# Windowed attention and ReGLU feed-forward: first q and k loads divided between two queues by partition half, tile 1 in two halves, wider weight pieces, and work reordered around the first output

## The chip, the cores and the metric

The kernel runs on one core of a Trainium2 chip. The time is device microseconds of one execution; a figure with three runs is their median. TensorE (PE) multiplies, VectorE (DVE) and ScalarE (ACT) work on the results, GpSimd (POOL) converts inputs to 16 bits, and SyncE (SP) and ACT each have a queue that issues transfers between the chip's memory (HBM) and the core's buffer (SBUF, 128 partitions).

## The reference

Attention in a causal window of 64 positions over q, k, v of 8 batches, 8 heads, 576 positions and 64 values, then a feed-forward layer on the 4608 tokens of width 512:

```python
scores = scale * np.matmul(q, k.transpose(0, 1, 3, 2))
mask = (rel >= 0) & (rel < window)            # window = 64
attn = softmax(np.where(mask, scores, -1e9))
x = np.matmul(attn, v)                        # heads side by side: (4608, 512)
gate = np.maximum(x @ w_gate, 0.0)            # w_gate, w_val: (512, 1536)
val = x @ w_val
return (gate * val @ w_out)                   # w_out: (1536, 512)
```

All inputs and the output are float32; the matmuls take 16-bit operands.

## The kernel before

**Attention units.** The 4608 tokens are cut into 24 units of 192 (three to a batch); u0 is the first. A unit's k, q and v are converted (`u_cast`, mostly on POOL), k and q transposed on DVE (`u_trans`, 4 instructions), and multiplied to scores (`u_st`, 32 matmuls into four PSUM tiles). ACT takes the exponential (`u_exp`, 4), DVE multiplies with the band mask (`u_mask`, 4), and PE forms sums and outputs (`u_pv`, 32 matmuls, each on half of the array's columns). ACT copies them out (`u_copy`, 4), and DVE makes the reciprocal and the normalised rows `xt` (`u_sum`, `u_back`, `u_norm`).

**Feed-forward tiles.** Before, tiles 0 and 1 hold 512 and 256 tokens and ten more hold 384 (`sizes`, line 66). For each of 12 blocks f of the hidden width and each of `wg` and `wv`, four matmuls make a PSUM tile `h` (line 323); ACT applies the relu (L314), DVE multiplies the two (`g_sb`, L317). Then, for each 128 tokens, 12 matmuls make `op` (L366), which ACT copies out. The four PSUM tiles of `f_ps` are shared by `h`, `op` and u1's scores.

**Loads.** `qk_load(b)` issues a batch's k and q as eight transfers: for each of them four groups g, a group filling 32 partitions (0 to 31, 32 to 63, 64 to 95, 96 to 127) with pieces of 512 bytes. For batch 0, even g go to SP's queue and odd g to ACT's (line 150). Then come v0 to v2, twelve chunks of `wg` and `wv` (512 KB each, pieces of 1 KB, lines 130 to 132), six of `wo` (pieces of 2 KB), batch 1's q and k, and v3 to v5, all on SP's queue. Six staging tiles `stg` take the weights; POOL converts each chunk.

**Order.** `Weaver` is a heap of planned times: program order on each engine is the order in which closures are popped, and `plan_unit` gives each step of a unit a planned time. Engines run their own instructions in that order and wait for data. Before, `ffn(0)` first makes f = 0 and 1 for the 384 tokens of u0 and u1 (`early`), then waits for u2, which fills the tile's last 128 tokens; `ready` stands ahead of each tile's other matmuls.

Of the kernel before, what the change touches and what calls it, by code (L numbers as in the profile page):

```python
# [9 lines left out]
FP32 = mybir.dt.float32  # L10
FP16 = mybir.dt.float16
# [31 lines left out]
def kernel(  # L43
# [79 lines left out]
    def w_load(wt, src, j, at):  # L123
        sr = src.rearrange("(c p) n -> p c n", p=128)
        if wt is wo:
            stg = stage.tile([128, 2, 512], FP32, name="stg", tag="stg")
            nc.sync.dma_start(stg, sr[:, 2 * j:2 * j + 2])
            dst = wo[:, 2 * j:2 * j + 2]
        else:
            stg = stage.tile([128, 4, 256], FP32, name="stg", tag="stg")  # L130
            nc.sync.dma_start(stg, sr[:, :, 256 * j:256 * j + 256])
            dst = wt[:, :, 256 * j:256 * j + 256]
# [13 lines left out]
    def qk_load(b):  # L146
        for name, src in (("k", k), ("q", q)):
            nat = a_in.tile([128, 2, UB, 3, 128], FP32, name=name + "n", bufs=2)
            for g in range(G):
                eng = nc.scalar if b == 0 and g % 2 else nc.sync  # L150
                eng.dma_start(  # L151
                    nat[32 * g:32 * g + 32].rearrange("p h u m e -> p (h u m) e"),
                    src[b, 2 * g:2 * g + 2].rearrange("h (m i j) d -> i (h m) (j d)", i=32, j=2))
            for i in range(UB):
                units.setdefault(UB * b + i, {})[name] = nat[:, :, i]

# [143 lines left out]
    def span(t):  # L300
        return sizes[t] * 23.4 / 384 + (1.8 if t == 0 else 3.6)

    def ready(t):
        while normed[0] * U < starts[t] + sizes[t]:
            W.pop()

    def ffn(t):
        n = sizes[t]
        xt = xt_tile(t)
        g_sb = g_sb_p.tile([128, NF, 512], FP16, name="g_sb")  # L310
        done = set()
# [4 lines left out]
        def gate(f, r_sb, h2):  # L316
            nc.vector.tensor_tensor(g_sb[:, f, 0:n], r_sb[:, 0:n], h2[:, 0:n], MUL)  # L317
            done.add(f)

        def hidden(h, wt, f, c0, c1):  # L320
            w_need(wt, f // 2)
            for c in range(NC):
                nc.tensor.matmul(h[:, c0:c1], wt[:, c, f * 128:f * 128 + 128], xt[:, c, c0:c1],  # L323
                                 start=(c == 0), stop=(c == NC - 1))
            W.clock += 4 * (c1 - c0) / 2400.0

        early = {}
        if t == 0:
            while normed[0] < 2:
                W.pop()  # L330
            for f in range(2):
                for i, wt in enumerate((wg, wv)):
                    early[f, i] = f_ps.tile([128, 512], FP32, name=f"h{i}", tag="h")
                    hidden(early[f, i], wt, f, 0, 2 * U)
        ready(t)

        for f in range(NF):
            for i, wt in enumerate((wg, wv)):
                W.advance(W.clock)
                if (f, i) in early:  # L340
                    h = early[f, i]
                    hidden(h, wt, f, 2 * U, n)
                else:
                    h = f_ps.tile([128, 512], FP32, name=f"h{i}", tag="h")
                    hidden(h, wt, f, 0, n)
                if i == 0:
                    r_sb = f_sb.tile([128, 512], FP32, name="r_sb")
# [4 lines left out]
        def evac(sub, op):  # L352
            o_sb = f_sb.tile([128, DM], FP32, name="o_sb")
            nc.scalar.copy(o_sb, op)  # L354
            nc.sync.dma_start(out[bass.ds(starts[t] + sub * 128, 128)], o_sb)

        for sub in range(n // 128):
            op = f_ps.tile([128, DM], FP32, name="op", tag="h")
            ss = bass.ds(sub * 128, 128)
            for f0 in range(0, NF, 4):  # L360
                W.advance(W.clock)
                for f in range(f0, f0 + 4):
                    while f not in done:
                        W.pop()
                    w_need(wo, f // 2)
                    nc.tensor.matmul(op, g_sb[:, f, ss], wo[:, f],  # L366
                                     start=(f == 0), stop=(f == NF - 1))
                W.clock += 4 * 512 / 2400.0
            W.at(W.clock, lambda sub=sub, op=op: evac(sub, op))

    with tc.manual_schedule():
        qk_load(0)
# [12 lines left out]
        for c in wo_chunks:
            W.at(t_load, lambda c=c, at=t_land: w_load(*c, at))
            t_load, t_land = t_load + 1.45, t_land + 1.45
        W.at(t_load, lambda: qk_load(1))
        for u in range(3, 6):
            W.at(t_load, lambda u=u: v_load(u))  # L390
# [44 lines left out]
```

## Time and profile before

| | us |
|---|---|
| median of 3 runs (lowest, highest) | 370.93 (369.5, 372.52) |
| the profiled execution, its own time | 371.01 |
| its span, first to last instruction | 369.2 |
| PE busy in the span | 333.5 (90%) |
| DVE, ACT, POOL busy | 239.5, 178.5, 94.3 |

Between the span and the execution's own time lie 1.8 us. The page cuts the span into 40 slices of 9.2 us; a digit is a busy share in tenths. A wait is idle time of an engine ahead of an instruction, put down to what released it. The chain of waits follows the work that ended last backwards, from each step to what it waited for. Matmuls overlap, so the distance between their starts is their cost, and the duration shown of one is longer.

### The profile page before, as it was taken

The numbers are of one execution on the slowest core, as the hardware profiler recorded it, in microseconds if no ns is written. First come the engines' busy times: TensorE is split into PE (matmuls) and PEld (weight loads), VectorE is DVE, ScalarE is ACT, GpSimd is POOL, SyncE is SP. The second block draws the span as 40 slices with busy tenths as digits, with TensorE's granted clock in tenths as the row PEclk, the third lists the DMA queues.
The fourth block names the chain that finished last, engine by engine and source line by source line (L and its number), as shares of the span: only waits on it lengthen the run. The fifth ranks groups of instructions, "written<-read, shape, count | busy, mean of one in ns | idle before, by whom it ended". The sixth has DMA issues, their size and how long they took to land.

```text
span 369.2 us, 7893 instructions
## 1 busy us (share of the span) xinstructions
PE 333.5 (90%) x3136; PEld 190.4 (52%) x3136; DVE 239.5 (65%) x439; ACT 178.5 (48%) x375; POOL 94.3 (26%) x114
## 2 busy tenths in 40 slices
PE   0154999698999999999999999999999999999996
PEld 0152544376465555565565555555555555555552
DVE  0598643968787578487587587588587487494330
ACT  1092332546556446545555555555554654653331
POOL 1486733604313222005213221006124121000000
PEclk9995999989999999999999999999999999999999
DMA  9999999995498520696696510694795600101102
GB/s 158 210 315 348 379 204 180 237 183 114 116 187 113 151 51 3 160 181 119 156 185 113 145 30 28 161 183 100 167 186 93 173 3 28 59 2 45 42 1 85
DMA packets 96901, 49.79 MB, mean 135 GB/s; under 512 B 47712, under 2 KB 90720, under 8 KB 96864
## 3 DMA queue, kind: packets, MB, share of 16 engines
q1 hardware_dynamic: 94496, 48.11, 63.2%
q10 hardware_dynamic: 2368, 1.18, 2.0%
q8 instruction: 24, 0.39, 0.5%
q14 instruction: 13, 0.11, 0.1%
HBM read 39.85 MB, written 9.44 MB: 134 GB/s over the span
## 4 chain that ended last, share of the span: by engine, by line
PE 84%; DVE 9%; DMA 4%; ACT 1%; issue 1%; ACTq 0%; DVEq 0%
PE h L323 51%; PE op L366 23%; PE pv L235 6%; DMA qn<-in_q_dram 4%; PE st L208 3%; DVE p L224 3%; DVE xt L270 2%; DVE sT L253 2%; DVE rs L261 1%; DVE qT L194 1%; ACT xs L248 1%; DVE rT L255 1%; DVE kT L194 0%; ACTq L151 0%; DVE g_sb L317 0%
## 5 line engine op out<-in xcount | busy, mean ns | idle before, releaser
L317 DVE TENSOR_TENSOR g_sb<-r_sb,h 128x384 f16<-128x384 f32 (+2 forms) x144 | 77.8, 546 | 74.8 <-PE h L323 73.5
L323 PE MATMUL h<-xt,wg 128*128 128x384 f16 (+3 forms) x584 | 119.2, 327 | 3.1 <-DVE xt L270 3.0
L323 PE MATMUL h<-xt,wv 128*128 128x384 f16 (+3 forms) x584 | 119.0, 327 | 0.3 <-DVE g_sb L317 0.3
L314 ACT ACTIVATE r_sb<-h 128x384 f32<-128x384 f32 (+2 forms) x144 | 71.6, 498 | 76.7 <-PE h L323 66.8
L366 PE MATMUL op<-wo,g_sb 128*128 128x512 f16 x432 | 97.0, 379 | 1.1 <-DVE g_sb L317 1.1
L323 PEld LDWEIGHTS <-wg 128*128 128x128 f16 x584 | 55.9, 99 | 43.3 <-issue 6.8
L323 PEld LDWEIGHTS <-wv 128*128 128x128 f16 x584 | 56.5, 99 | 38.0 <-issue 1.1
L366 PEld LDWEIGHTS <-g_sb 128*128 128x128 f16 x432 | 41.3, 98 | 49.4 <-issue 1.3
L220 ACT ACTIVATE p<-st 128x512 f16<-128x512 f32 x96 | 52.2, 607 | 11.3 <-PE st L208 11.1
L248 ACT COPY xs<-pv 128x384 f32<-128x384 f32 x96 | 39.5, 501 | 25.0 <-PE pv L235 25.0
L224 DVE TENSOR_TENSOR p<-p,mask 128x512 f16<-128x512 f16 x96 | 45.4, 492 | 9.0 <-ACT p L220 7.9
L354 ACT COPY o_sb<-op 128x512 f32<-128x512 f32 x36 | 21.1, 587 | 60.7 <-PE op L366 60.7
L182 POOL CAST k<-kn 128x768 f16<-128x768 f32 x24 | 23.1, 964 | 81.0 <-DMA kn<-in_k_dram 65.3
L235 PE MATMUL pv<-p,v 128*64 128x128 f16 x384 | 25.8, 232 | 10.3 <-DVE p L224 10.1
L182 POOL CAST q<-qn 128x768 f16<-128x768 f32 x23 | 20.2, 878 | 57.8 <-DMA qn<-in_q_dram 30.7
L175 POOL CAST v<-vn 128x1024 f16<-128x1024 f32 x16 | 17.2, 1076 | 66.6 <-PE pv L235 48.4
L194 DVE STREAM_TRANSPOSE kT<-k 128x384 f16<-128x384 f16 x48 | 27.7, 590 | 9.7 <-POOL k L182 8.7
L253 DVE STREAM_TRANSPOSE sT<-xs 128x768 f32<-128x768 f32 x24 | 23.1, 961 | 15.8 <-ACT xs L248 15.8
L208 PE MATMUL st<-qT,kT 32*128 32x128 f16 x768 | 16.8, 223 | 17.3 <-DVE qT L194 17.3
L194 DVE STREAM_TRANSPOSE qT<-q 128x384 f16<-128x384 f16 x48 | 26.6, 582 | 7.0 <-POOL q L182 3.8
L235 PEld LDWEIGHTS <-v 128*64 128x64 f16 x384 | 17.7, 115 | 19.1 <-issue 16.9
L235 PE MATMUL pv<-p,ones 128*64 128x128 f16 x384 | 25.1, 229 | 0.0
(26 smaller groups left out, 123.6 us busy)
## 6 DMA issues: line engine op xcount, KB each, us to landing
vn<-in_v_dram SPq DMA_DIRECT2D x40, 256.0 KB, 5.3
out_dram<-o_sb SPq DMA_DIRECT2D x36, 256.0 KB, 2.0
kn<-in_k_dram SPq DMA_DIRECT2D x30, 288.0 KB, 7.9
qn<-in_q_dram SPq DMA_DIRECT2D x30, 288.0 KB, 9.2
stg<-in_moe_w_gate_dram SPq DMA_DIRECT2D x6, 512.0 KB, 7.8
stg<-in_moe_w_val_dram SPq DMA_DIRECT2D x6, 512.0 KB, 8.1
stg<-in_moe_w_out_dram SPq DMA_DIRECT2D x6, 512.0 KB, 7.5
vn<-in_v_dram SPq DMA_DIRECT2D x8, 128.0 KB, 8.2
```

The lines of the kernel that those rows point to most:

```text
L182: nc.gpsimd.tensor_copy(c16, src)
L194: nc.vector.transpose(dst.rearrange("p h (m i j) -> p h m j i", i=32, j=2), src)
L208: nc.tensor.matmul(d["st"][g][:, (2 * hh + w) * 128:(2 * hh + w + 1) * 128], kT[rows, dh, hh, ks + 128 * w:ks + 128 * w + 128], d["qT"][ro ...
L220: nc.scalar.activation(d["p"][g].rearrange("p h c -> p (h c)"), d["st"][g], ACT.Exp, scale=scale)
L224: nc.vector.tensor_tensor(p, p, mask.rearrange("p w c -> p (w c)")[:, None, :].to_broadcast([128, 2, 256]), MUL)
L235: nc.tensor.matmul(pv[64 * e:64 * e + 64, s, 64 * w:64 * w + 128], d["v16"][:, w, 2 * g + e] if s == 0 else (ones0 if u % UB == 0 and w == ...
L248: nc.scalar.copy(d["xs"][:, g], d["pv"][g])
L253: nc.vector.transpose(sT.rearrange("p g b c -> p g (b c)"), d["xs"][:, :, 1])
L314: nc.scalar.activation(r_sb[:, 0:n], h1[:, 0:n], ACT.Relu)
L317: nc.vector.tensor_tensor(g_sb[:, f, 0:n], r_sb[:, 0:n], h2[:, 0:n], MUL)
L323: nc.tensor.matmul(h[:, c0:c1], wt[:, c, f * 128:f * 128 + 128], xt[:, c, c0:c1], start=(c == 0), stop=(c == NC - 1))
L366: nc.tensor.matmul(op, g_sb[:, f, ss], wo[:, f], start=(f == 0), stop=(f == NF - 1))
```

## The change

Names of units, tiles and blocks are as above.

- **First loads.** Batch 0's k and q: groups 0 and 1 (partitions 0 to 63) go to SP's queue, groups 2 and 3 (64 to 127) to ACT's. All batches issue g in the order 0, 2, 1, 3.
- **Weights.** A chunk of `wg` or `wv` is now 256 rows by 512 columns, in pieces of 2 KB, where it was 512 rows by 256 columns. Its size and the number of chunks stay. Four chunks serve f = 0 to 3, where two served f = 0 and 1.
- **Later loads.** v2 stands behind the first four weight chunks. Batch 1's q and k come in two goes: the first third (what u3 needs) in 16 small transfers, then v3, then the rest in 16, then v4 and v5.
- **Tiles.** All twelve have 384 tokens, two units each. Tile 1's hidden part is done in two halves of 192 (u2, then u3). Between them stands tile 0's output, now f by f over three `op` tiles at once (`output_by_rows`), where it was one `op` after another.
- **u2** has later planned times: its masks stand behind the normalisation of u1, its `pv` behind f = 0 and 1 of tile 0.
- **`heat`:** 14 matmuls of 256 columns on the mask, whose result is not read, behind u2's scores and ahead of tile 0.

```diff
-    sizes = [512, 256] + [384] * 10
+    TT = 2 * U
...
-            stg = stage.tile([128, 4, 256], FP32, name="stg", tag="stg")
-            nc.sync.dma_start(stg, sr[:, :, 256 * j:256 * j + 256])
+            cs, ns = slice(2 * (j % 2), 2 * (j % 2) + 2), slice(512 * (j // 2), 512 * (j // 2) + 512)
+            dst, part = wt[:, cs, ns], sr[:, cs, ns]
+        stg = stage.tile([128, 2, 512], FP32, name="stg")
+        nc.sync.dma_start(stg, part)
...
+    def queue(b, g):
+        return nc.scalar if b == 0 and g >= G // 2 else nc.sync
...
-                eng = nc.scalar if b == 0 and g % 2 else nc.sync
...
+            for i in range(G):
+                g = i // 2 + 2 * (i % 2)
+                rows = slice(32 * g, 32 * g + 32)
+                if blocks is None:
+                    queue(b, g).dma_start(
...
+                else:
+                    m0, m1 = blocks
+                    for h in range(2):
+                        queue(b, g).dma_start(
+                            nat[rows, h, m0:m1],
...
+    def output_by_rows(t):
+        ops = [op_tile() for _ in range(TT // 128)]
+        for f in range(NF):
+            W.advance(W.clock)
+            for sub, op in enumerate(ops):
+                out_mm(t, op, sub, f)
...
-        plan_unit(2, 18.3, (7.6, 10.9, 13.7), (9.0, 12.8), 1.6, 3.8, 5.3, 6.2, 7.7, 0.4)
-        plan_unit(3, 51.0, (44.5, 47.5, 48.5), (46.5, 49.0), 0.8, 1.5, 3.4, 4.5, 6.4, 0.5)
...
+        plan_unit(2, 18.3, (7.6, 10.9, 24.5), (9.0, 12.8), 1.6, 5.5, 8.0, 9.0, 10.4, 0.4)
+        plan_unit(3, 50.0, (44.0, 46.5, 47.5), (45.5, 48.2), 0.8, 1.5, 3.4, 4.5, 6.4, 0.5)
...
+        heat = f_ps.tile([128, 512], FP32, name="heat", tag="h")
+        for _ in range(14):
+            nc.tensor.matmul(heat[:, 0:256], mask[:, 0], mask.rearrange("p w c -> p (w c)"),
+                             start=True, stop=True)
...
+        ready(2)
+        hidden(0, 0, TT)
+        ready(3)
+        hidden(1, 0, U)
+        output_by_rows(0)
+        ready(4)
+        hidden(1, U, TT)
+        output(1)
```

On DVE, from u1's normalisation (`sT`, `rT`, `rs`, `xt`; u0's stands ahead of it, behind the eight masks of u0 and u1) to what follows, before:

```order
L253 STREAM_TRANSPOSE sT<-xs 128x768
L255 RECIPROCAL rT<-sT 128x24
L224 TENSOR_TENSOR p<-p,mask 128x512
L261 STREAM_TRANSPOSE rs<-rT 128x768
L224 TENSOR_TENSOR p<-p,mask 128x512 x2
L270 TENSOR_TENSOR xt<-xs,rs 128x4x192
L224 TENSOR_TENSOR p<-p,mask 128x512
L253 STREAM_TRANSPOSE sT<-xs 128x768
```

and now:

```order
L271 STREAM_TRANSPOSE sT<-xs 128x768
L273 RECIPROCAL rT<-sT 128x24
L279 STREAM_TRANSPOSE rs<-rT 128x768
L285 TENSOR_TENSOR xt<-xs,rs 128x4x192
L242 TENSOR_TENSOR p<-p,mask 128x512 x4
L331 TENSOR_TENSOR g_sb<-r_sb,h_459 128x384
```

Three masks of u2 stood inside u1's normalisation and the fourth behind it; all four now stand behind it, and the first gate comes ahead of u2's normalisation.

On SP's queue, from the `wo` chunks to the next batch's loads, before:

```order
L127 DMA stg<-in_moe_w_out_dram 128x2x512 x6
L151 DMA kn<-in_k_dram 32x18x128 x4
L151 DMA qn<-in_q_dram 32x18x128 x4
L164 DMA vn<-in_v_dram 64x8x64
L164 DMA vn<-in_v_dram 128x8x64 x5
L355 DMA out_dram<-o_sb 128x512 x3
```

and now:

```order
L131 DMA stg<-in_moe_w_out_dram 128x2x512 x6
L170 DMA kn<-in_k_dram 32x3x128 x8
L170 DMA qn<-in_q_dram 32x3x128 x8
L182 DMA vn<-in_v_dram 64x8x64
L182 DMA vn<-in_v_dram 128x8x64
L170 DMA kn<-in_k_dram 32x6x128 x8
L170 DMA qn<-in_q_dram 32x6x128 x8
L182 DMA vn<-in_v_dram 128x8x64 x4
```

The same bytes are moved in 32 transfers where eight did it, u3's part first, v3 between the two goes.

On DVE, around u3, before (k_725 and q_742 are u4's, k_867 is u5's; the twelve gates of tile 0 and u3's own transposes stand ahead):

```order
L194 STREAM_TRANSPOSE kT_95<-k_725 128x2x3x2x32
L224 TENSOR_TENSOR p<-p,mask 128x512 x2
L194 STREAM_TRANSPOSE kT_95<-k_725 128x2x3x2x32
L224 TENSOR_TENSOR p<-p,mask 128x512 x2
L194 STREAM_TRANSPOSE qT<-q_742 128x6x2x32 x2
L253 STREAM_TRANSPOSE sT<-xs 128x768
L255 RECIPROCAL rT<-sT 128x24
L261 STREAM_TRANSPOSE rs<-rT 128x768
L194 STREAM_TRANSPOSE kT_95<-k_867 128x2x3x2x32
L270 TENSOR_TENSOR xt<-xs,rs 128x4x192
L317 TENSOR_TENSOR g_sb<-r_sb,h_955 128x256
```

and now (k_857 and q_882 are u4's, k_1028 is u5's; the gates ahead are those of tile 1's first half):

```order
L331 TENSOR_TENSOR g_sb<-r_sb,h_894 128x192
L212 STREAM_TRANSPOSE kT_95<-k_857 128x2x3x2x32
L242 TENSOR_TENSOR p<-p,mask 128x512 x3
L212 STREAM_TRANSPOSE kT_95<-k_857 128x2x3x2x32
L242 TENSOR_TENSOR p<-p,mask 128x512
L212 STREAM_TRANSPOSE qT<-q_882 128x6x2x32 x2
L271 STREAM_TRANSPOSE sT<-xs 128x768
L273 RECIPROCAL rT<-sT 128x24
L279 STREAM_TRANSPOSE rs<-rT 128x768
L285 TENSOR_TENSOR xt<-xs,rs 128x4x192
L212 STREAM_TRANSPOSE kT_95<-k_1028 128x2x3x2x32
```

The order around u3 stays nearly the same; what moved is what stands ahead of it, the gates of a 384-token tile 0 and of half a tile 1 in place of those of a 512-token tile 0.

## Rows read from the trace of the kernel before

**Rows 1.** The page: span, PE's busy tenths and its granted clock in 40 slices.

```profile
span 369.2 us, 7893 instructions
PE   0154999698999999999999999999999999999996
PEclk9995999989999999999999999999999999999999
```

**Rows 2.** The chain of waits, first 90 us: start, length, what.

```profile
2.41 13.02 DMA qn<-in_q_dram
...
29.39 0.60 DVE p L224
...
30.88 0.95 DVE p L224 x2
31.83 1.71 DVE xt L270
...
38.32 0.98 DVE xt L270
...
82.25 1.01 PE pv L235 x32
```

**Rows 3.** DMA issues by line: queue, count, KB of one, median us to landing.

```profile
kn<-in_k_dram ACTq DMA_DIRECT2D x2, 288.0 KB, 6.6
```

**Rows 4.** Stretches: bounds, length, busy PE, PEld, DVE, ACT, POOL; clock, DMA share, GB/s.

```profile
7.00:8.00 1.00, 0.00 (x0) 0.00 (x0) 0.00 (x0) 0.00 (x0) 0.00 (x0) 1.00 1.25 174
...
11.00:12.00 1.00, 0.00 (x0) 0.04 (x1) 1.00 (x3) 0.00 (x0) 0.54 (x2) 1.00 1.23 286
...
24.00:34.00 10.00, 2.91 (x71) 2.22 (x68) 9.86 (x13) 4.98 (x12) 7.29 (x8) 0.67 1.10 348
41.00:45.00 4.00, 4.00 (x21) 1.82 (x19) 2.06 (x4) 1.27 (x3) 3.09 (x4) 1.00 1.05 386
48.00:57.00 9.00, 9.00 (x43) 4.05 (x42) 3.71 (x6) 2.98 (x5) 2.38 (x3) 1.00 1.24 187
```

**Rows 5.** PE in order of time: start, us from first start to last end, what.

```profile
35.34 1.46 PE L323 MATMUL h<-xt,wg 128*128 128x384 f16 x4
...
64.68 0.63 PE L208 MATMUL st<-qT,kT 32*128 32x128 f16 x32
65.23 2.76 PE L366 MATMUL op<-wo,g_sb 128*128 128x512 f16 x12
...
74.75 0.64 PE L323 MATMUL h<-xt,wg 128*128 128x256 f16 x4 [2.70 <-DVE xt L270]
75.18 1.06 PE L323 MATMUL h<-xt,wv 128*128 128x256 f16 x4
...
78.59 0.60 PE L323 MATMUL h<-xt,wv 128*128 128x256 f16 x4
79.03 0.60 PE L323 MATMUL h<-xt,wg 128*128 128x256 f16 x4
...
97.11 0.81 PE L323 MATMUL h<-xt,wg 128*128 128x384 f16 x4 [0.29 <-DVE xt L270]
...
98.41 0.82 PE L323 MATMUL h<-xt,wv 128*128 128x384 f16 x4
99.07 0.81 PE L323 MATMUL h<-xt,wg 128*128 128x384 f16 x4
...
357.61 7.93 PE L366 MATMUL op<-wo,g_sb 128*128 128x512 f16 x36
```

**Rows 6.** SP's queue in order of time: start, length of the issues, what.

```profile
0.81 0.93 SPq L151 DMA_DIRECT2D kn<-in_k_dram  x2
...
42.20 5.80 SPq L151 DMA_DIRECT2D kn<-in_k_dram  x4
```

**Rows 7.** DVE's gates by form: line, operation, shape, count; busy us, mean ns, idle before.

```profile
L317 DVE TENSOR_TENSOR g_sb<-r_sb,h 128x384 f16<-128x384 f32 x120 | 64.7, 545 | 59.9 <-PE h L323 59.2 <-ACT r_sb L314 0.4
...
L317 DVE TENSOR_TENSOR g_sb<-r_sb,h 128x256 f16<-128x256 f32 x12 | 4.9, 406 | 4.1 <-PE h L323 3.4 <-ACT xs L248 0.7
```

More of the change, by code (lines that the diff above doesn't have):

```diff
@@ L65 @@
     scale = 1.0 / float(D) ** 0.5
-    sizes = [512, 256] + [384] * 10
-    starts = [sum(sizes[:i]) for i in range(len(sizes))]
-    assert sum(sizes) == NT
+    TT = 2 * U
+    assert NT % TT == 0 and TT % 128 == 0
     consts = ctx.enter_context(tc.tile_pool(name="consts", bufs=1))
@@ L297, in plan_unit, with ready, hidden @@
         W.at(T + norm + 2.0, lambda: u_norm(u))
[L300 to L304, printed above, removed]
+    gs = {}
+    def ready(n):
+        while normed[0] < n:
             W.pop()
-    def ffn(t):
-        n = sizes[t]
+    def hidden(t, c0, c1):
+        if t not in gs:
+            gs[t] = g_sb_p.tile([128, NF, TT], FP16, name="g_sb"), set()
+        g_sb, done = gs[t]
         xt = xt_tile(t)
-        g_sb = g_sb_p.tile([128, NF, 512], FP16, name="g_sb")
-        done = set()
+        n = c1 - c0
         def relu(r_sb, h1):
@@ L316, in gate @@
         def gate(f, r_sb, h2):
[L317 to L335, printed above, removed]
+            nc.vector.tensor_tensor(g_sb[:, f, c0:c1], r_sb[:, 0:n], h2[:, 0:n], MUL)
+            if c1 == TT:
+                done.add(f)
         for f in range(NF):
@@ L339, in ffn @@
                 W.advance(W.clock)
[L340 to L345, printed above, removed]
+                w_need(wt, f)
+                h = f_ps.tile([128, 512], FP32, name=f"h{i}", tag="h")
+                for c in range(NC):
+                    nc.tensor.matmul(h[:, 0:n], wt[:, c, f * 128:f * 128 + 128], xt[:, c, c0:c1],
+                                     start=(c == 0), stop=(c == NC - 1))
+                W.clock += 4 * (n + 7) / 2400.0
                 if i == 0:
-                    r_sb = f_sb.tile([128, 512], FP32, name="r_sb")
+                    r_sb = f_sb.tile([128, TT], FP32, name="r_sb")
                     W.at(W.clock, lambda r_sb=r_sb, h=h: relu(r_sb, h))
@@ L350, in ffn, with out_mm, out_evac, evac @@
                     W.at(W.clock, lambda f=f, r_sb=r_sb, h=h: gate(f, r_sb, h))
-        def evac(sub, op):
+    def out_mm(t, op, sub, f):
+        g_sb, done = gs[t]
+        while f not in done:
+            W.pop()
+        w_need(wo, f)
+        nc.tensor.matmul(op, g_sb[:, f, bass.ds(sub * 128, 128)], wo[:, f],
+                         start=(f == 0), stop=(f == NF - 1))
+        W.clock += 519 / 2400.0
+    def out_evac(t, op, sub):
+        def evac():
             o_sb = f_sb.tile([128, DM], FP32, name="o_sb")
             nc.scalar.copy(o_sb, op)
[L355 to L369, printed above, removed]
+            nc.sync.dma_start(out[bass.ds(t * TT + sub * 128, 128)], o_sb)
+        W.at(W.clock, evac)
+    def op_tile():
+        return f_ps.tile([128, DM], FP32, name="op", tag="h")
+    def output(t):
+        for sub in range(TT // 128):
+            op = op_tile()
+            for f in range(NF):
+                if f % 4 == 0:
+                    W.advance(W.clock)
+                out_mm(t, op, sub, f)
+            out_evac(t, op, sub)
+    def output_by_rows(t):
+        ops = [op_tile() for _ in range(TT // 128)]
+        for f in range(NF):
+            W.advance(W.clock)
+            for sub, op in enumerate(ops):
+                out_mm(t, op, sub, f)
+        for sub, op in enumerate(ops):
+            out_evac(t, op, sub)
     with tc.manual_schedule():
+        qk_tiles(0)
         qk_load(0)
@@ L385 @@
[L385 to L390, printed above, removed]
+        chunks = [(wt, src, 2 * j + i) for j in range(3)
+                  for wt, src in ((wg, moe_w_gate), (wv, moe_w_val)) for i in range(2)]
+        chunks += [(wo, moe_w_out, j) for j in range(6)]
+        t_load, t_land = 6.0, 17.5
@@ L404 @@
+        ready(2)
[6 more added lines that the diff above has]
+        output(1)
+        for t in range(2, NU // 2):
+            ready(2 * t + 2)
+            hidden(t, 0, TT)
+            output(t)
         W.drain()
```

76 lines of the change are left out of this document (40 added, 36 removed).

## The prediction

> **What bounds the kernel now.** I read the page first. The span is 369.2 us; PE is near nine tenths busy in every slice from the fifth on, but for slices 8 and 10 [rows 1]. PE therefore sets the time, and a change can gain only ahead of its dense stretch and in the holes up to about 100 us. The granted clock says where PE, though busy, ran slowly: slice 4 stands at half, slice 9 below full [rows 1].
>
> The chain of waits says what is late at the start: for 13.02 us it is the first q, until 15.43; then DVE, whose normalisation of u1 ends at 31.83 + 1.71 = 33.5 with u2's masks inside it; then u2, whose last rows `xt` end at 39.30 [rows 2]. PE in order of time gives the marks that I count between. Tile 0 starts at 35.34, its first four matmuls taking 1.46 (half clock, since 0.81 is the usual), and tile 2 starts at 97.11 [rows 5]. From tile 2 on both kernels have the same tiles, units and order of work, so I forecast when tile 2 starts.
>
> In the kernel before, what PE does between the marks costs, by the distance between starts: four matmuls of 384 columns 0.66 (98.41 to 99.07), of 256 0.44 (78.59 to 79.03), so 0.22 for each 128; a unit's scores 0.55 (64.68 to 65.23); 36 output matmuls 7.93 [rows 5]; a unit's `pv` 1.01 [rows 2]. Tile 0 of 512 (24 x 0.88 = 21.1), tile 1 of 256 (24 x 0.44 = 10.6), 72 output matmuls (15.9), three scores and three `pv` (4.7) make 52.3, of 97.11 - 35.34 = 61.8. So 9.5 us are lost there: some 2 in tile 0's cold start and its wait for u2, 2.7 waiting for u3 at 74.75 [rows 5], 1.7 in the half clock right behind it (four groups from 75.18 to 78.59 take 3.41 and not 1.75) [rows 5], and some 3 in smaller waits on DVE.
>
> **The change part by part.**
>
> *First loads.* Eight transfers of 288 KB [rows 3] are 2.36 MB; in 13.02 us [rows 2] that is 181 GB/s. Both queues begin in partitions 0 to 63 and then both go to 64 to 127. The rate is 174 GB/s in the stretch from 7 to 8 and 286 from 11 to 12 [rows 4]. I read the second as a moment at which the queues, a transfer apart, wrote to different halves; no row says so. If halves are the limit, the new split holds the better rate throughout. Bounds: 181 (no gain) and 286 (8.3 us). I take 250, two thirds of the way, since short drops at the ends of transfers should remain: 9.4 us, a gain of **3.6** (0 to 4.7). k, at half of the bytes, then also comes earlier, and its transposes on DVE are out of the way in time. The rates tell for the split, but a page speaks against it. The Trainium skill (SBUF — State Buffer, "Can I just issue two DMAs to hit both halves?") says that two transfers at a time, one at partition 0 and one at 64, gave only 6% over one. By that the gain is 13.02 - 13.02/1.06 = 0.7; the 286 [rows 4] is more than it allows, but lasts about a microsecond. It is a rival below.
>
> *u1 ahead of u2's masks.* The chain has 0.60 and 0.95 for the three masks inside u1's normalisation [rows 2]: 1.55 go. u1's rows are ready at 33.54 - 3.6 - 1.55 = **28.4**, and tile 0 starts there, where it started at 35.34, because its matmuls no longer stand behind u2's `pv`. Nor does it wait for u2, which now has the rest of tile 0 to finish.
>
> *Paid back.* u2's `pv` moves into the stream, 1.0. `heat` costs nothing, since PE has only DVE to wait for then; its cover is PE's idle time ahead of tile 0 (busy 5 and 4 tenths in slices 3 and 4, 18.5 us [rows 1]), against at most 14 matmuls of 256 columns at half clock, 14/4 of 0.85 = 3.0 (the four groups below 75.18 [rows 5]). Without cover it would cost those 3.0, or half at full clock. Whether it keeps the clock up across what idles behind it, no row shows. Before, PE did u2's scores and part of its `pv` in about that stretch and the clock still fell [rows 1]. I take a start at half clock, 1.7 lost, as in the stretch after 75.18 [rows 5]; bounds 0 and 3.4, two such stretches.
>
> *Weights.* Pieces of 1 KB come at 348 GB/s (24 to 34), of 2 KB at 386 (41 to 45, mostly `wo`) [rows 4]. Twelve chunks gain 6.3 MB x (1/348 - 1/386) = 1.8 us of transfer. I price that at nothing. What hides it: with q in at 11.8, 1.44 MB of v at the slowest rate shown (187 [rows 4]) and 1.36 for a chunk, eight chunks are in at about 30 and twelve at 36; f = 4 needs the eight at 28.4 + 1.7 + 1.0 + 8 x 0.66 = 36.4, f = 8 the twelve at 41.7. If v2's delay or the coarser need (four chunks before any f) took that cover, each late chunk would cost 1.4 us.
>
> *Tiles 0 and 1.* From tile 0's start to tile 2 PE now does: tile 0 of 384, 24 x 0.66 = 15.8; u2's `pv` 1.0; twice half a tile, 24 x 0.33 = 7.9 each; 72 output matmuls 15.9; three scores and three `pv` 4.7. That is 53.2. The 96 more matmuls of narrower tiles are in it, by columns; a fixed cost of each I take from 0.66 against 3 x 0.22 as nothing.
>
> *Waits.* u3's scores stand behind 6 output matmuls. Their place is 28.4 + 1.7 + 15.8 + 1.0 + 7.9 + 1.3 = 56.1. Between them and half a tile that needs u3 stand 30 output matmuls, u3's `pv` and u4's scores, 8.2 us. In the old trace the way from scores to rows was 74.75 - 64.68 = 10.1 [rows 5], with DVE waiting for k and q of u4 on it. I take 9 and a wait of **0.8** (0 to 3). A short wait leaves the clock up, so the 1.7 behind it go too. From there to tile 2, DVE is as full as before: 12 gates at about 0.34 (the step from 406 to 545 ns for 128 columns [rows 7], halved below 406) against 12 at 0.41, and u4's and u5's work the same. The same stretch lost 22.36 (74.75 to 97.11) - 18.6 (10.6 + 0.55 + 2.0 + 5.4 for 24 output matmuls) - 1.7 of clock = 2.1. I take **2.6**, as the half tile gives less PE time to hide gates at its start (1.5 to 4.5).
>
> *Batch 1's loads.* 32 transfers do what eight did. SP's first issues take 0.93 for two; later four take 5.80, with 288 KB each moving at 187 GB/s, which is 1.58 apiece [rows 3, 4, 6]: that is data, not issue. At 0.47 each, 16 small transfers take 7.5; six `wo` chunks end at 36 + 8.2 = 44, so u3's q is there at about 51.5 and is wanted at about 54. v3 (2 us) and u4's k (4.2 at 187) follow by 58. u4's first transpose of k stands ahead of u3's masks on DVE, and those could begin, by my estimate, a little over 1 us behind u3's scores, at about 57.4; behind the masks PE's `pv` waits. So this has no margin if the issues don't run ahead of the data, and the 3 in the bound above holds that. I price it at nothing: SP, with no `out` ahead of these loads, can issue them while `wo` is still moving.
>
> **Sum.** 28.4 + 53.2 + 1.7 + 0.8 + 2.6 = 86.7 for tile 2, against 97.11: 10.4 less. The profiled execution took 371.01 (0.08 over the median), so **360.6**.
>
> **The rivals.**
>
> *The split gives nothing.* The limit might be the 512-byte pieces or the way they lie in HBM: the later loads on one queue, with the same pieces, ran at only 187 [rows 4]. Against it stands the 286. Everything behind shifts by 3.6: 364.2. By the 6% of the page named above it would be 363.5.
>
> *The clock stays up.* `heat` works, or the stretch falls well: 1.7 less, 358.9. Against it: the stretch without matmuls behind it is longer than it is.
>
> *DVE and ACT become the bound in tiles 0 and 1.* 24 gates of 192 cost 8.1 and 12 of 384 6.5, where 12 of 512 and 12 of 256 cost 8.2 and 4.9 by the same step [rows 7]: 1.5 more. With u3 late by 2 and the stretch behind at 4.5, that adds 3.1 and perhaps the clock's 1.7: 363.7 to 365.4.
>
> *Small transfers make it slower.* If each of the small ones cost the 1.58 of a large one [rows 6], u3's 16 end at 44 + 16 x 1.58 = 69, not 51.5. u3's scores go from 56 to 72 at the earliest, PE having nothing else once 6 output matmuls are done: 16 later, 376 or more, since u4's loads are later still. It turns the gain into a loss from about 1.3 each (10.4 + 2.5 of margin, over 16, above 0.47). For it: I see no row with pieces this few. Against it: 0.47 for issues that waited for nothing.
>
> **How the numbers follow.** Chances: the forecast 0.50 (alone 358.5 to 362.5), no gain by the split 0.22, the clock up 0.12, DVE and ACT 0.08, small transfers 0.05, several holes left as they were, within 1%, 0.03. The time is that of the likeliest, 360.6. The range 356.5 to 366.0 takes in the best rate of loading together with a clock that stays up (360.6 - 1.1 - 1.7, and a little less wait), and at its other end no gain of the split with 2 us more of waits. About 1% is what a measurement of this kernel can tell from no change, so 367.2 and 374.6 are the edges: faster 0.87 (the first four cases have 0.92, less 0.05 for several of them adding up), within 0.07, slower 0.06.
>
> **What would show it.** q's wait in the chain ends at about 11.8 (at 15 if the split does nothing). Tile 0's first matmul is at about 28.4, and the clock's row there says whether `heat` helped. No PE wait longer than 1 us stands between 29 and 55; a wait of about 0.8 for `xt` of u3 near 65. Gates, in tile 1's second half, are what PE waits for. Tile 2 starts near 87. The forecast fails if tile 0 waits for weights, if u3's scores wait for q on POOL, or if the holes behind tile 0 come back in another place.

## The result and the profile after

The changed kernel takes 361.75 us (median of 4 runs, 361.44 to 362.14) against 371.25 us before in the same session: the ratio is 0.9748, with a 95% interval of 0.9705 to 0.979. Forecast were 360.6, between 356.5 and 366.0. Its profiled execution took 361.96 us. The total was forecast well; several of its terms were not, and in part they cancel.

The page of the changed kernel, its span, PE's busy tenths and its granted clock in 40 slices:

```profile
span 360.2 us, 8167 instructions
PE   0276999999999999999999999999999999999995
PEclk9998999999999999999999999999999999999999
```

Against [rows 1], the holes of slices 8 and 10 are gone, and the only dip of the clock left is a small one in slice 4.

The chain of waits of the changed kernel (start, length, what), to be read against [rows 2]:

```profile
2.41 10.46 DMA qn<-in_q_dram
...
17.20 7.24 DVE p L242 x8
...
29.95 1.85 DVE xt L285
...
36.28 1.01 PE pv L253 x32
...
60.16 0.56 PE st L226 x32
```

q is in 2.56 us earlier (10.46 for 13.02). But eight masks stand in the chain with 7.24 us. The same row of the kernel before was this:

```profile
19.75 4.73 DVE p L224 x8
```

The forecast had carried that length over silently. PE of the changed kernel in order of time, to be read against [rows 5]:

```profile
31.93 1.44 PE L341 MATMUL h<-xt,wg 128*128 128x384 f16 x4 [3.02 <-DVE xt L285]
33.16 1.49 PE L341 MATMUL h<-xt,wv 128*128 128x384 f16 x4
34.44 1.19 PE L341 MATMUL h<-xt,wg 128*128 128x384 f16 x4
35.47 0.81 PE L341 MATMUL h<-xt,wv 128*128 128x384 f16 x4
...
69.49 0.49 PE L341 MATMUL h<-xt,wg 128*128 128x192 f16 x4 [0.51 <-DVE xt L285]
...
79.61 0.49 PE L341 MATMUL h<-xt,wv 128*128 128x192 f16 x4 [0.43 <-DVE g_sb L331]
...
88.83 0.81 PE L341 MATMUL h<-xt,wg 128*128 128x384 f16 x4
```

Tile 0 starts at 31.93 (35.34 before), its first three groups at half clock (1.2 of 2.4 GHz; from 32 to 35.5 the granted clock is 0.54 on the mean); tile 2 starts at 88.83 (97.11 before), 8.28 us earlier. From there to the end it is 360.2 - 88.83 = 271.4 us, where it was 369.2 - 97.11 = 272.1. To within 0.1 us, these 8.28 + 0.7 are the whole difference of the two profiled executions, 371.01 - 361.96 = 9.05.

### The profile page after: what moved, and what is told of

Same layout as the page of the kernel before. It is cut to its first block, busy times and chain, and to the rows that moved or that the text cites. A ratio compares the mean times of both kernels' runs of the same rounds, so it can differ in the third digit from the quotient of the medians.

```text
span 360.2 us, 8167 instructions
## 1 busy us (share of the span) xinstructions
PE 333.6 (93%) x3230; PEld 196.6 (55%) x3230; DVE 238.2 (66%) x450; ACT 179.4 (50%) x387; POOL 94.7 (26%) x114
## 4 chain that ended last, share of the span: by engine, by line
PE 86%; DVE 8%; DMA 3%; ACT 1%; issue 1%; ACTq 0%; DVEq 0%
PE h L341 51%; PE op L355 25%; PE pv L253 6%; PE st L226 3%; DMA qn<-in_q_dram 3%; DVE p L242 2%; DVE xt L285 1%; DVE rs L279 1%; DVE g_sb L331 1%; DVE sT L271 1%; DVE qT L212 1%; ACT xs L266 0%; ACTq L164 0%; DVE kT L212 0%; DVE rT L273 0%
## 5 line engine op out<-in xcount | busy, mean ns | idle before, releaser
L341 PE MATMUL h<-xt,wg 128*128 128x384 f16 (+1 forms) x624 | 120.4, 316 | 3.7 <-DVE xt L285 3.5
L341 PE MATMUL h<-xt,wv 128*128 128x384 f16 (+1 forms) x624 | 120.1, 316 | 0.4 <-DVE g_sb L331 0.4
L331 DVE TENSOR_TENSOR g_sb<-r_sb,h 128x384 f16<-128x384 f32 (+1 forms) x156 | 79.1, 512 | 61.9 <-PE h L341 55.0
L328 ACT ACTIVATE r_sb<-h 128x384 f32<-128x384 f32 (+1 forms) x156 | 73.5, 472 | 77.1 <-PE h L341 53.0
L355 PE MATMUL op<-wo,g_sb 128*128 128x512 f16 x432 | 95.7, 380 | 0.0
L341 PEld LDWEIGHTS <-wg 128*128 128x128 f16 x624 | 58.8, 98 | 40.0 <-POOL wv L134 3.3
L341 PEld LDWEIGHTS <-wv 128*128 128x128 f16 x624 | 58.5, 98 | 34.7 <-issue 1.1
L242 DVE TENSOR_TENSOR p<-p,mask 128x512 f16<-128x512 f16 x96 | 46.2, 503 | 30.3 <-ACT p L238 29.4
L200 POOL CAST q<-qn 128x768 f16<-128x768 f32 x23 | 19.4, 843 | 56.4 <-DMA qn<-in_q_dram 42.0
L226 PEld LDWEIGHTS <-kT 32*128 32x128 f16 x768 | 12.3, 98 | 23.3 <-issue 11.3
```

Source lines behind the costliest of these rows:

```text
L200: nc.gpsimd.tensor_copy(c16, src)
L226: nc.tensor.matmul(d["st"][g][:, (2 * hh + w) * 128:(2 * hh + w + 1) * 128], kT[rows, dh, hh, ks + 128 * w:ks + 128 * w + 128], d["qT"][ro ...
L242: nc.vector.tensor_tensor(p, p, mask.rearrange("p w c -> p (w c)")[:, None, :].to_broadcast([128, 2, 256]), MUL)
L328: nc.scalar.activation(r_sb[:, 0:n], h1[:, 0:n], ACT.Relu)
L331: nc.vector.tensor_tensor(g_sb[:, f, c0:c1], r_sb[:, 0:n], h2[:, 0:n], MUL)
L341: nc.tensor.matmul(h[:, 0:n], wt[:, c, f * 128:f * 128 + 128], xt[:, c, c0:c1], start=(c == 0), stop=(c == NC - 1))
```

## The experiments

Each is the changed kernel with the edit shown, unless said otherwise. Columns: median and range of the runs, ratio to the kernel before on the same chip with its interval, and the starts of tile 0 and tile 2 in the profiled execution. The kernel before had medians of 369.9 to 372.0 us in the sessions, so ratios are compared, not medians; 0.001 is 0.37 us. The two starts are those of one execution each. e5, e7 and e10 have the changed kernel's program up to tile 0 and start it at 31.97, 31.64 and 30.95, against 31.93: so much can lie between two executions of the same work.

| kernel | us (range) | ratio (95%) | tile 0 | tile 2 |
|---|---|---|---|---|
| changed kernel | 361.75 (361.44-362.14) | 0.9748 (0.9705-0.979) | 31.93 | 88.83 |
| e1_inphase | 364.28 (363.63-365.04) | 0.9835 (0.9798-0.9871) | 34.41 | 91.92 |
| e2_crossed | 362.58 (362.56-363.31) | 0.9793 (0.976-0.9826) | 31.70 | 89.41 |
| e3_casts_wait | 361.11 (360.66-362.16) | 0.9752 (0.9716-0.9789) | 29.79 | 89.04 |
| e4_no_heat | 363.47 (362.96-364.77) | 0.9824 (0.9781-0.9867) | 31.97 | 89.84 |
| e5_batch1_whole | 363.55 (362.82-364.31) | 0.9783 (0.975-0.9817) | 31.97 | 90.37 |
| e6_1k_pieces | 363.38 (363.18-363.66) | 0.9779 (0.9748-0.9809) | 31.76 | 90.09 |
| e7_tile1_whole | 370.91 (369.28-372.86) | 0.9985 (0.996-1.0011) | 31.64 | 97.36 |
| e8_u2_early | 366.57 (365.75-367.02) | 0.9868 (0.9831-0.9905) | 35.11 | 91.60 |
| e10_v_first | 362.32 (360.76-363.3) | 0.9741 (0.9704-0.9778) | 30.95 | 87.62 |
| e11_wait_v_first | 361.6 (360.24-362.22) | 0.9721 (0.9688-0.9754) | 29.44 | 89.07 |
| e12_more_heat | 361.78 (361.39-361.99) | 0.9727 (0.9696-0.9758) | 29.24 | 88.47 |
| e13_u4_later | 361.76 (360.83-362.57) | 0.9734 (0.9701-0.9767) | 29.11 | 87.70 |

### Is it the halves that speed up the first loads?

e1_inphase gives the two queues alternating groups, as before, in the changed kernel's order of issue:

```diff
-        return nc.scalar if b == 0 and g >= G // 2 else nc.sync
+        return nc.scalar if b == 0 and g % 2 else nc.sync
```

> The changed kernel with batch 0's groups given to the queues by parity again (SP 0 and 2, ACT 1 and 3), so that both queues write partitions 0 to 63 first and 64 to 127 then. Theory (a half of the partitions limits what both queues can write into it): the wait for the first q, which ended at 12.87 in the changed kernel and at 15.43 before, ends at 15.0 to 15.6 again, the rate near 4 to 8 us falls to about 175 GB/s, and the time is 2 to 2.6 over the changed kernel's 361.75: about 364. Rival (which queue takes which half does not matter, the gain came from v2 and the weights standing further back or from the order 0, 2, 1, 3): 12.9 and 361.8.

e2_crossed has the same split by parity, but ACT's queue takes its groups in the other order, so that the queues are mostly in opposite halves:

```diff
+                g = (0, 3, 2, 1)[i] if b == 0 else i // 2 + 2 * (i % 2)
```

> Groups by parity as in e1_inphase, but ACT takes its groups in the order 3, 1 where SP takes 0, 2: each queue visits both halves, but at any time they are in different ones. Theory (halves): as fast as the changed kernel, q's wait ends at 12.6 to 13.4, time 361.3 to 362.4. Rival (a queue has to stay in one half): as e1_inphase, 15.0 to 15.6 and about 364.

Stretches of the changed kernel (bounds, length, busy PE, PEld, DVE, ACT, POOL; clock, DMA share, GB/s):

```profile
4.00:6.00 2.00, 0.00 (x0) 0.00 (x0) 0.00 (x0) 0.46 (x2) 0.00 (x0) 1.00 1.22 236
6.00:8.00 2.00, 0.00 (x0) 0.00 (x0) 0.00 (x0) 0.00 (x0) 0.00 (x0) 1.00 1.25 216
8.00:10.00 2.00, 0.00 (x0) 0.06 (x1) 0.71 (x2) 0.00 (x0) 1.57 (x2) 1.00 1.21 283
```

and of e1_inphase:

```profile
4.00:6.00 2.00, 0.00 (x0) 0.00 (x0) 0.00 (x0) 0.60 (x2) 0.00 (x0) 1.00 1.24 189
6.00:8.00 2.00, 0.00 (x0) 0.00 (x0) 0.00 (x0) 0.00 (x0) 0.00 (x0) 1.00 1.26 176
8.00:10.00 2.00, 0.00 (x0) 0.00 (x0) 0.00 (x0) 0.00 (x0) 0.70 (x1) 1.00 1.24 189
```

The wait for q in the chain of e1_inphase:

```profile
2.41 12.94 DMA qn<-in_q_dram
```

and of e2_crossed:

```profile
2.41 11.11 DMA qn<-in_q_dram
```

In e1 the wait for q is nearly that of the kernel before; in e2 it is 11.11 us, in the changed kernel 10.46 (10.36 to 10.69 in e4, e6, e8, e10 and e13, which have the split too). Same bytes, same pieces, same two queues: the half that each queue is in at the time decides most of it. e2 stays 0.65 us behind the changed kernel, its wait ends at 13.52 where 13.4 was the latest expected, and why was not tried. Over the whole wait, 2.36 MB come at 182 GB/s in phase and at 226 apart. With tile 0 and tile 2 later by 2.5 and 3.1 us in e1, the split's part of the gain is shown. The rule that speaks against it, in the Trainium skill (SBUF — State Buffer, "Can I just issue two DMAs to hit both halves?"), that a second transfer in the other half adds 6%, does not hold for these transfers: apart they are 24% faster than two queues in one half, and 21% faster than the 187 GB/s at which one queue moved such pieces [rows 4].

### Why tile 0 still starts 3.5 us later than forecast

The masks of u0 and u1 (count; shortest, median, longest ns; when), up to 25 us, before:

```profile
L224 DVE TENSOR_TENSOR p<-p,mask x8: 382/412/1252, 19.6 to 23.2; 128x512 f16<-128x512 f16 x8
```

in the changed kernel:

```profile
L242 DVE TENSOR_TENSOR p<-p,mask x8: 386/1250/1252, 17.1 to 24.0; 128x512 f16<-128x512 f16 x8
```

POOL in order of time in the kernel before:

```profile
20.46 1.23 POOL L175 CAST v<-vn 128x1024 f16<-128x1024 f32 x1
22.99 1.22 POOL L175 CAST v<-vn 128x1024 f16<-128x1024 f32 x1 [1.30 <-PE pv L235]
24.15 1.23 POOL L135 CAST wg<-stg 128x1024 f16<-128x1024 f32 x1
```

and in the changed kernel:

```profile
17.90 1.23 POOL L193 CAST v<-vn 128x1024 f16<-128x1024 f32 x1
19.08 2.40 POOL L134 CAST wg<-stg 128x1024 f16<-128x1024 f32 x2
21.43 2.40 POOL L134 CAST wv<-stg 128x1024 f16<-128x1024 f32 x2
24.93 1.04 POOL L193 CAST v<-vn 128x1024 f16<-128x1024 f32 x1 [1.11 <-PE pv L253]
```

A mask takes 1.25 us while a cast runs beside it, and 0.41 alone. Before, v2's cast stood ahead of the first weight cast and waited for u0's `pv`: POOL idled, and four masks ran alone. With v2 moved behind four weight chunks, casts fill POOL up to the last mask: five masks take 1.25 where two did, and 3 x 0.84 = 2.5 us is what the eight grew by. The Trainium skill has the rule that the prediction lacked (SBUF — State Buffer, "Who interferes with whom"): a vector instruction with two inputs in SBUF contends with a GpSimd instruction that reads there. The trace agrees. The test holds POOL back with a tiny copy that reads u1's last masked tile:

```diff
+        scr = consts.tile([128, 2], FP16)
+        def guard():
+            nc.gpsimd.tensor_copy(scr, units[1]["p"][3][:, 0, 0:2])
+        W.at(17.45, guard)
```

> The changed kernel with one small copy on POOL, ahead of the first weight cast, that reads u1's last masked tile, so that no weight cast runs beside the masks of u0 and u1. Theory (a mask on DVE and a cast on POOL take turns, 1.25 us for the pair, where a mask alone takes 0.41): the eight masks, 7.24 us in the chain of the changed kernel, take about 4 (the exponentials' pace), tile 0 starts at 28.5 to 29.2 and not at 31.93, and the time falls by 2.5 to 3.5, to about 358.8. Rival 1 (masks wait for something else): masks as long as before, 361.8. Rival 2 (the casts, now later, hold tile 0 or slow the normalisation as much): tile 0 waits for wg or wv, 361 to 364.

The masks of e3_casts_wait:

```profile
L242 DVE TENSOR_TENSOR p<-p,mask x8: 385/410/1250, 17.6 to 21.2; 128x512 f16<-128x512 f16 x8
```

The collision is confirmed: tile 0 starts at 29.79, 2.1 us earlier (28.5 to 29.2 was expected). Yet tile 2 starts at 89.04, and the time is that of the changed kernel. Of the 2.1 us, 0.7 went into the clock: with a longer wait ahead of it, tile 0's first four groups take 5.05 (29.79 to 34.84), where the changed kernel's take 4.35 (31.93 to 36.28). What took the rest is followed up below.

The same collision also moves tile 0 from one execution to the next. u1's `xt` has two inputs in SBUF as well. In the changed kernel a cast begins just ahead of it, at 29.93:

```profile
29.93 1.04 POOL L134 CAST wv<-stg 128x1024 f16<-128x1024 f32 x1 [0.32 <-DMA stg<-in_moe_w_val_dram]
```

and `xt`, from 29.95 on, takes 1.85 (the chain above). In e10_v_first, whose program is the same up to there, `xt` begins between two casts. The chain of e10_v_first:

```profile
29.85 0.97 DVE xt L285
```

The cast behind it, from 30.13 on, takes 1.57 instead, and tile 0 starts 1.0 us earlier than in the changed kernel.

### What each other part is worth

e8_u2_early puts u2 back to its old planned times, but for its value cast:

```diff
-        plan_unit(2, 18.3, (7.6, 10.9, 24.5), (9.0, 12.8), 1.6, 5.5, 8.0, 9.0, 10.4, 0.4)
+        plan_unit(2, 18.3, (7.6, 10.9, 23.4), (9.0, 12.8), 1.6, 3.8, 5.3, 6.2, 7.7, 0.4)
```

> u2 is planned as in the kernel before (masks right behind its exponentials and between u1's, value sums ahead of tile 0, v's cast at 23.4); the rest is the changed kernel. The prediction gave u2's later place 1.55 us of DVE in front of tile 0. Theory A (the masks stand ahead of u1's normalisation, and each costs 0.4 to 1.25 us depending on a cast beside it): tile 0 starts 1.6 to 5 us later than 31.93, less the 1.0 us of value sums no longer in the stream: 362.5 to 366 us. Rival B (u1's normalisation is bound elsewhere, by ACT's copies): tile 0 at about 32, 361 to 362 us.

Tile 0 starts at 35.11, and the ratio rises by 0.012 (4.5 us). With u2's masks inside u1's normalisation again, u1's rows are ready at 33.31, 1.5 us later than in the changed kernel. The chain of e8_u2_early:

```profile
31.60 1.71 DVE xt L285
```

The other 1.8 us are u2's `pv`, which again stands ahead of tile 0: PE stands 2.47 us on u2's last mask there:

```profile
34.54 0.42 PE L253 MATMUL pv<-p,v 128*64 128x128 f16 x4 [2.47 <-DVE p L242]
```

e4_no_heat leaves the 14 warm-up matmuls out.

> The changed kernel without the 14 heat matmuls. Theory (they end 3 us ahead of tile 0 and do not keep the clock up): tile 0 starts at 31.9 again, the clock is at half for its first groups as now, 361.3 to 362.3. Rival (they shorten the half clock from several stretches to one): tile 0's first groups stay at half for one stretch of 3.4 us more, 363.5.

PE of e4_no_heat:

```profile
31.97 1.44 PE L341 MATMUL h<-xt,wg 128*128 128x384 f16 x4 [5.58 <-DVE xt L285]
...
35.77 1.35 PE L341 MATMUL h<-xt,wv 128*128 128x384 f16 x4
```

Tile 0 starts at the same time, so `heat` does lie under idle time. Without it a fourth group is slow, and tile 2 starts 1.0 us later (2.8 us by the ratio, whose interval overlaps the changed kernel's, and 1.7 by the medians). The half clock is read here from the lengths, 1.35 to 1.48 where 0.81 is usual; the granted clock of this trace shows no fall. What the warm-up is worth differs between executions: in e7 and e10, with the changed kernel's program up to there, tile 0 starts at full clock. PE of e10_v_first:

```profile
30.95 0.81 PE L341 MATMUL h<-xt,wg 128*128 128x384 f16 x4 [1.76 <-DVE xt L285]
```

So it shortens the half clock, and in some executions none is left behind it.

e7_tile1_whole does tile 1 in one piece after tile 0's output:

```diff
-        ready(3)
-        hidden(1, 0, U)
         output_by_rows(0)
         ready(4)
-        hidden(1, U, TT)
+        hidden(1, 0, TT)
```

> Tile 1 in one piece of 384 columns after tile 0's output, gated on u3 (tile 0, output of tile 0, tile 1, output of tile 1); first loads, heat, weights and u2's plan as in the changed kernel. Theory A (the two halves cover u3): without the first half (about 10.2 us of matmuls) ahead of it, TensorE ends tile 0's output about 10 us earlier and stands waiting for u3, which comes at about 69.5 as before or up to 4 us earlier, since its scores then wait for less; tile 2 then at 92 to 99 instead of 88.8, and 365 to 372 us. Rival B (the halves only move the wait, u3 comes as much earlier): 361 to 363 us.

PE of e7_tile1_whole:

```profile
56.63 0.62 PE L226 MATMUL st<-qT,kT 32*128 32x128 f16 x32
61.28 0.32 PE L253 MATMUL pv<-p,v 128*64 128x128 f16 x2 [4.02 <-POOL v L190]
...
68.07 1.44 PE L341 MATMUL h<-xt,wg 128*128 128x384 f16 x4 [2.24 <-DVE xt L285]
```

All of the gain is gone: ratio 0.9985. Tile 0 starts as early as in the changed kernel, but PE then has no work of its own while u3 comes. Between 57 and 68 it is busy 3.6 of 11 us, and it comes out of that at half clock. u3's rows are ready 1.4 us earlier than in the changed kernel, which is all that rival B offers. So the earlier start counts only because half of tile 1 is there to fill the wait for u3. Part of that wait is POOL's order, in which u4's key cast stands ahead of u3's value cast (the 4.02 above, and the last part below); e7 with that order turned round was not run, so its price holds for the order as it is.

e5_batch1_whole loads batch 1's q and k whole:

```diff
-        W.at(t_load, lambda: qk_load(1, (0, 3)))
+        W.at(t_load, lambda: qk_load(1))
         W.at(t_load, lambda: v_load(3))
-        W.at(t_load + 5.0, lambda: qk_load(1, (3, 9)))
```

> Batch 1's k and q are loaded whole again (eight transfers of 288 KB, k then q, before v3), where the changed kernel loads the first third of each (16 transfers of 96 KB), then v3, then the rest. Everything else is the changed kernel. Theory A (the small first third is what brings u3 in time): the whole q ends about 1.6 MB later at 187 to 250 GB/s than its first third, so u3's scores, its gate on tile 1's second half and tile 2 come 5 to 8 us later, less the 0.5 us of slack that PE waited there already; 366 to 369 us. Rival B (the loads' order does not matter, the stream catches up): 361.8 us, tile 2 at 88.8 as in the changed kernel.

e6_1k_pieces takes the old chunks of the weights:

```diff
-            cs, ns = slice(2 * (j % 2), 2 * (j % 2) + 2), slice(512 * (j // 2), 512 * (j // 2) + 512)
-            dst, part = wt[:, cs, ns], sr[:, cs, ns]
+            ns = slice(256 * j, 256 * j + 256)
+            dst, part = wt[:, :, ns], sr[:, :, ns]
...
+        chunks = [(wt, src, j) for j in range(6) for wt, src in ((wg, moe_w_gate), (wv, moe_w_val))]
```

> wg and wv in the chunks of the kernel before (4 x 256 columns, pieces of 1 KB, six chunks each), casts in the same form; the rest is the changed kernel. The prediction priced the 2 KB pieces at nothing: the weights' stretch then runs at about 348 instead of 387 GB/s and lasts about 1.8 us longer, hidden behind tile 0: 361.8 us. Rival (after the first loads, the transfers are the second limit, so u3's inputs come 1.8 us later and PE waits for them): 363 to 363.6 us, with u3's gate on tile 1's second half at 71 or later (69.5 in the changed kernel).

Both are a little slower, by 0.0035 and 0.0031 (1.3 and 1.2 us). Their intervals overlap that of the changed kernel, but tile 2 starts 1.5 and 1.3 us later in the rows, and no run of either is as fast as the slowest of the changed kernel. Not all of this need be the loads' doing: in e1 and e2, which differ from the changed kernel in the first loads alone, the way from tile 0 to tile 2 is 0.6 and 0.8 us longer as well. For e5, theory A holds in sign, its 5 to 8 us do not: u3's scores come only about half a microsecond later (some wait for qT at 60.6). For e6 the rival's time came, but not by its way. In the stretch from 28 to 37 us, 1 KB pieces bring 351 GB/s and 2 KB pieces 387; yet u3's scores, at 60.49, wait for no transfer, and u3's half tile starts at 70.10, not at 71 or later. The rows show DVE's work beside casts that now come at other times: u2's `xt` takes 1.75 (1.28 in the changed kernel), and PE waits here:

```profile
43.54 0.81 PE L341 MATMUL h<-xt,wv 128*128 128x384 f16 x4 [0.36 <-DVE g_sb L331]
...
70.10 0.49 PE L341 MATMUL h<-xt,wg 128*128 128x192 f16 x4 [0.73 <-DVE xt L285]
...
73.10 0.49 PE L341 MATMUL h<-xt,wv 128*128 128x192 f16 x4 [0.53 <-DVE g_sb L331]
```

### Where the rest of e3's 2.1 us went, and whether more is to be had

In both kernels u4's key cast stands ahead of u3's value cast on POOL, and waits for the rest of batch 1. POOL of e3_casts_wait:

```profile
60.29 0.82 POOL L200 CAST k<-kn 128x768 f16<-128x768 f32 x1 [7.08 <-DMA qn<-in_q_dram]
...
62.58 0.69 POOL L191 CAST v<-vn 128x512 f16<-128x512 f32 x1
```

e10_v_first turns that order round, e11_wait_v_first does so together with e3's edit, and e12_more_heat is e11 with `range(30)` for the warm-up:

```diff
-        plan_unit(3, 50.0, (44.0, 46.5, 47.5), (45.5, 48.2), 0.8, 1.5, 3.4, 4.5, 6.4, 0.5)
+        plan_unit(3, 50.0, (44.0, 46.5, 46.9), (45.5, 48.2), 0.8, 1.5, 3.4, 4.5, 6.4, 0.5)
```

> The changed kernel with one number moved: u3's value cast stands on POOL ahead of u4's key cast (planned at 46.9 instead of 47.5, between u3's query cast and u4's key cast). In the changed kernel u4's key cast waits 5.90 us for its transfer until 58.81, and u3's three value instructions queued behind it end at 61.4, although v3 is loaded ahead of that transfer. Theory A (u3's value sums hang on POOL's order): they come up to 1 us earlier than 64.1, u3's gate on tile 1's second half falls from 0.51 to nothing; 361.0 to 361.5 us. Rival B (u3's masks end the wait for the value sums anyway): 361.8 us, the same wait of 0.5.

> Both edits together: the weight casts wait for u1's masks (as in e3_casts_wait) and u3's value cast stands ahead of u4's key cast. e3 brought tile 0 2.1 us earlier and gave it back at u3, whose value sums waited for POOL at 63.3. Theory A (POOL's order was what gave it back): tile 2 1 to 2 us earlier than in e3_casts_wait (89.04), 359.5 to 360.3 us. Rival B (batch 1's transfers give it back: u3's query lands no earlier than before): tile 2 at 88.5 to 89, 361.1 us.

> As e11_wait_v_first, with 30 warm-up matmuls in place of 14: their wait before tile 0 was 4.1 us in e3_casts_wait, and 16 more take 1.7 us at full and 3.4 at half clock. Theory A (the length of the idle stretch ahead of tile 0 decides whether it starts at half clock): tile 0 starts at the same time with a wait under 2.5 us and at full clock, which saves 1.5 to 2.6 us against e11. Rival B (the half clock follows from the light work before it, warm-up or not): tile 0's first three groups are slow as before, the time of e11.

The order of POOL was a cause in e3, but not the only one. In e10 u3's values are cast by 55.7, and PE still waits 0.82 for u3's rows; its time is no better, which is rival B's case. (That its tile 0 is early and at full clock is not the edit's doing, as said above.) In e11 tile 0 starts 2.5 us earlier than in the changed kernel, and tile 2 at 89.07. What still holds u3 back is DVE, where u4's key transpose stands ahead of u3's masks, as it did in e3 (where DVE stood 2.96 us on it). DVE of e11_wait_v_first:

```profile
60.42 0.61 DVE L212 STREAM_TRANSPOSE kT<-k 128x384 f16<-128x384 f16 x1 [3.31 <-POOL k L200]
60.92 1.05 DVE L242 TENSOR_TENSOR p<-p,mask 128x512 f16<-128x512 f16 x3
```

and PE of it:

```profile
68.86 0.49 PE L341 MATMUL h<-xt,wg 128*128 128x192 f16 x4 [1.72 <-DVE xt L285]
```

The longer warm-up of e12 leaves the time where it is: the wait ahead of tile 0 shrinks to 2.57 us, tile 0's first group runs at full clock, then the clock falls all the same. Its theory A, which wanted under 2.5 us, is not borne out. e13_u4_later adds to e11 that u4's transposes stand behind u3's work:

```diff
-        plan_unit(4, 58.0)
-        plan_unit(5, 66.0)
+        plan_unit(4, 60.5, (49.0, 50.0, 51.0), (53.4, 58.5))
+        plan_unit(5, 68.3)
```

> e11_wait_v_first with u4 and u5 planned 2.5 and 2.3 later and u4's transposes moved on DVE: its keys' behind u3's masks, its queries' behind u3's normalisation. In e11 DVE stood 3.31 us on u4's key cast, which waits for the rest of batch 1, with u3's four masks, ready from about 58.9, queued behind it until 60.92; u3's gate on tile 1's second half then cost 1.72 us. Theory A (the in-order DVE queue hands the late transfers of u4 to u3): u3's masks start at about 59, its gate costs nothing, tile 2 1.5 to 2 us earlier than in e11 (89.06); 359.5 to 360.3 us. Rival B (u3 comes earlier, but u4 and u5 come later and tile 2 waits for them): 361 to 362 us.

u3's masks now start at 58.56, PE reaches u3's half tile at 66.67 instead of 68.86, and what comes late next is u5. PE of e13_u4_later:

```profile
66.67 0.49 PE L341 MATMUL h<-xt,wg 128*128 128x192 f16 x4 [1.06 <-DVE xt L285]
...
87.70 0.81 PE L341 MATMUL h<-xt,wg 128*128 128x384 f16 x4 [1.14 <-DVE xt L285]
```

Theory A is right for u3's masks, though PE still waits 1.06 us for u3's rows, and rival B for the time: 361.76 us. None of e3 and e10 to e13 is faster than the changed kernel by more than their intervals; whether one of them is ahead by half a microsecond stays open.

## Why the prediction came out right

- **First loads: right in kind, too large.** Forecast 3.6, measured 2.56. The assumed 250 GB/s was not held; the mean was 226, with 216 in one stretch and 283 in the next. The rival without a gain falls with e1 and e2.
- **u1's normalisation: the step that failed.** Taking u2's masks out of it was right, and e8 shows both of its parts: the masks at the 1.5 that were priced, and `pv` out of tile 0's way at another 1.8. But 28.4 was worked out with the eight masks ahead at their old length. They took 7.24 for 4.73, since the moved loads put POOL's casts beside three more of them. 33.54 - 2.56 - 1.55 + 2.51 is 31.94; u1's rows were ready at 31.80, and tile 0 started at 31.93.
- **Warm-up and clock: right, in this execution.** It cost nothing. Forecast were 1.7 lost at half clock; the first three groups took 3.54 (31.93 to 35.47) and not 1.98, so 1.6. The open question is answered in part by e4: the warm-up helps. That the clock was low at all is in part chance: in e7 and e10 the same program started tile 0 at full clock, which is the rival of the clock that stays up.
- **Weights at nothing: wrong by about 1.2.** Tile 0 never waited for a chunk, as forecast. But in e6 tile 2 came 1.3 us later. Later chunks move POOL's casts beside other work of DVE; how much of the loss is that, and how much the later transfers of u3 and u4, is not shown.
- **Work and waits up to tile 2: work right, waits too large.** From tile 0 to tile 2 it is 56.9, so beside the 53.2 of work 3.7 are lost where 5.1 were forecast: 1.6 of clock, 0.5 for u3 (0.8), and 1.6 that remain for small waits (2.6). The 96 more matmuls are 80 in the trace, which the sum by columns does not feel. DVE did not become the bound; its one wait of note in tile 1 is 0.43.
- **Batch 1's small transfers: right.** SP issues the first eight in 7.90 from 38.20 on, 0.99 each, which is more than the 0.47 assumed and less than the 1.58 of that rival; but it began while `wo` was still moving, and u3's q was cast from 52.08 on, with 51.5 forecast for its landing. e5 shows a small gain where I had priced nothing.
- **From tile 2 on: 0.7 missed.** I took it as unchanged; why it is 271.4 in nearly all kernels with tile 1 in halves, and 272.1 before and in e7, was not tried.

With the signs: 360.6 + 3.5 (tile 0) - 1.4 (waits) - 0.7 = 362.0, against 361.96. The prediction was right on most of its mechanisms and lacked one, masks and casts that hold each other up. That it came within 1.4 us is partly luck: it was 3.5 too early at tile 0 and 2.1 too slow behind it.

The parts do not add up singly. Undone one at a time, they cost, by ratios that are each uncertain by 1 to 2 us, 3.2 (split), 4.5 (u2), 8.8 (halves of tile 1), 2.8 (warm-up), 1.3 and 1.2 us: 21.8 in all, more than twice the 9.4 that the change gains. They lie in one chain, in which undoing one takes the benefit from the others; e7 alone takes it all.

## What to carry to other kernels

An earlier start is worth only what the next late input leaves of it: before pricing a gain at the head, find work for the engine to do while that input comes (half a tile here), and look for what stands ahead of it in the in-order queues of POOL and DVE. When a change moves loads, ask on which engine their casts will now run beside what, since the neighbour's duration is not fixed. Two queues that load narrow groups of partitions should be in opposite halves at the same time.

## What the runs showed of the hardware

- Two queues with transfers of 32 partitions each ran from 4 to 10 us at 176 to 189 GB/s while both were in one half of the partitions (e1), and at 216 to 283 while they were in different halves (the changed kernel).
- A 128x512 mask on DVE with both inputs in SBUF took 1.25 us beside a 128x1024 cast on POOL, and 0.41 alone; the cast took about 1.2 beside it, and 1.04 alone. The two engines went step by step. The one that began first kept its time: u1's `xt` took 0.97 ahead of a cast of 1.57 (e10), and 1.85 behind a cast of 1.04.
- The clock followed neither from the warm-up alone nor from the length of the wait behind it. In e7 and e10, after 14 warm-up matmuls and 2.38 and 1.76 us of waiting, tile 0 ran at full clock from the start; in e2, with 2.31 us, it fell within the first group; in e12, with 30 of them and 2.57 us, it ran one group at full clock and then fell; in the changed kernel, with 14 and 3.02 us, it started at half.
